# A state-space scan and a feed-forward block in one kernel: the first state products re-ordered, one weight step pulled ahead, one step of the second y put in one place

## The chip, the cores and the metric

The kernel runs on one core of a Trainium2 chip. The core has a matrix engine (TensorE, PE in the profile, with its weight loads as PEld), a vector engine (VectorE, DVE), a scalar engine (ScalarE, ACT), a general engine (GpSimd, POOL) and a queue engine that issues transfers (SyncE, SP). Each works through its own list in order and waits for others by semaphores. The metric is the device time of one execution in microseconds (us). Three timed executions of the kernel before gave 348.64, 349.24 and 348.39 us, so the median is 348.64 us.

## The reference

Two parts follow each other. The first is a chunked linear recurrence for 4 batches of 8 heads, 768 steps long, with head width 32 and state width 16. For each chunk of the sequence

```
M       = (C B^T) * exp(cum_i - cum_j), lower triangle       # inside the chunk
y_intra = M x
y_inter = (C state) * exp(cum_i)                             # from the state carried in
state   = exp(sum) * state + sum_j B_j x_j exp(cum_last - cum_j)
```

where `cum` is the running sum of log a. The second part takes y as 3072 rows of 256 numbers and computes `g = h / (1 + exp(-1.702 h))` with `h = y w_in` (256 to 2048), and then `g w_out` (2048 to 256). The two weight matrices arrive as 64-bit floats and are used as 32-bit ones; the kernel does this conversion itself.

## The kernel before, in words

The 3072 rows are cut into six groups of 512 rows (`g` = 0 to 5). A group is two pairs of 128-row chunks; the kernel works on chunks as two sides of 64 rows each (side 0 and side 1). For each group the kernel forms yT, the transposed y of the group (128 x 2 x 512, the two halves of the 256 columns are `t` = 0 and 1), then 16 hidden blocks of 128 columns, then the output. Group 0 uses plain products; from group 1 on, the kernel uses a scheme of seven products in place of eight (the lines L948, L958 and L1053), which does not change here.

**First y.** `finish(range(PG))` (L1207) forms y of group 0 out of two sums in four banks of the accumulator memory, `y0_0` to `y0_3`, one for each pair of side and column half: bank `2 t + i` holds side `i`, half `t`. `intra` (L830) adds M x; a filler product (`dense(4, ...)`, 256 columns, result unused) follows; `inter` (L810) adds C times the carried state. `inter` is made of small products with 32 rows and 64 columns. The four row groups `r` = 0 to 3 of the array hold two heads each, and `r // 2` is the column half `t`. ScalarE then copies each bank to yT (L856, four copies, t outer and side inner). The first hidden product needs both copies of half 0, the second those of half 1.

**Weights.** The 64-bit words of w_in and w_out come in pieces. `PIECES` 0 to 3 are two hidden blocks each (blocks 0 to 7), 4 and 5 four blocks each (8 to 11, 12 to 15), 6 to 9 are w_out. Each piece goes through

- `fields(i)` on VectorE (L192, L195): take the exponent and the mantissa out of the high word; it is the first step that needs the piece's transfer;
- `clamp(i)` on ScalarE (L203, L204): bring the exponent into range;
- `rounded(i)` on VectorE (L208): add the low word to the mantissa;
- `join(i)` on VectorE (L222 and L228): put sign, exponent and mantissa together and write the 32-bit weights. For piece 4 it is done in two halves, so that blocks 8 and 9 come before 10 and 11. After pieces 1 and 5, `join` also issues the transfer of piece 6 or 9.

`narrow(i)` (L235) is `rounded(i)`, then `fields(i + 1)`, then `join(i)`.

**Hidden blocks of group 0.** `hidden(0, f)` (L887) is four PE instructions (two products, each in two passes) into one bank of a ring of four (`bank`, L581, tag "ff"), then a Silu on ScalarE (L896) that empties it. With the allocations in program order, block 9 takes the bank that block 5 used. The table `in_hidden` (L1228 to L1236) says what is put behind which block: `narrow(4)` and then `clamp(5)` behind block 4, `narrow(5)` behind 6, `pick_a` (two ScalarE copies, L366) behind 6, `clamp(6)` and `fan_all` (PE, L412) behind 9, and so on. The lists of all engines are put in that program order by `in_order` (L21), so ScalarE does `clamp(5)` after the Silu of block 4 and before that of block 5.

**The second y.** `in_project` says the same for the output products of group 0 (L990, four instructions for each `f`). Behind the products before f = 9 stand `score` (L682) and `gain` (L713, the increments of the state) of the second group. `gain` writes a bank that `since_start` on VectorE (L667) must have read. `finish(pairs, (0,))` puts `inter` of group 1 ahead of f = 13 and `finish(pairs, (1,))` puts `intra` and the two copies to yT (L871) ahead of f = 15.

**fold_ident(1)** (L333) fills the second half of a constant that `decay` (L402) uses from group 1 on. It is one VectorE instruction.

Of the kernel before, what the change touches and what calls it, by code (L numbers as in the profile page):

```python
# [35 lines left out]
def kernel(  # L36
# [151 lines left out]
    def fields(i):  # L188
        hi, cols = bits[i][1], slice(0, PIECES[i][2] * DM)
        mantissa[i] = wide.tile([P, PN], U32, tag="m", name=f"m{i}")[:, cols]  # L190
        power[i] = wide.tile([P, PN], U32, tag="p2", name=f"p2{i}")[:, cols]
        nc.vector.tensor_scalar(out=power[i], in0=hi, scalar1=0x7FF00000, scalar2=None,  # L192
                                op0=ALU.bitwise_and)

        nc.vector.tensor_scalar(out=mantissa[i], in0=hi, scalar1=0x000FFFFF,  # L195
                                scalar2=0x00100000, op0=ALU.bitwise_and, op1=ALU.bitwise_or)
# [9 lines left out]
    def rounded(i):  # L206

        nc.vector.scalar_tensor_tensor(out=mantissa[i].bitcast(FP32), in0=bits[i][0],  # L208
                                       scalar=2.0 ** -32, in1=mantissa[i],
                                       op0=ALU.mult, op1=ALU.add)  # L210
# [4 lines left out]
    def join(i, parts=1):  # L215

        name, f, n = PIECES[i]
        n //= parts
        low, m, p2 = bits.pop(i)[1], mantissa.pop(i), power.pop(i)
        for k in range(parts):  # L220
            cols, fs = slice(k * n * DM, (k + 1) * n * DM), slice(f + k * n, f + (k + 1) * n)
            nc.vector.scalar_tensor_tensor(out=p2[:, cols], in0=low[:, cols], scalar=0x80000000,  # L222
                                           in1=p2[:, cols], op0=ALU.bitwise_and, op1=ALU.bitwise_or)
            if name == "in":
                dst, h = w_in[:, fs].rearrange("p f k e -> p (f k e)").unsqueeze(1), 1
            else:
                dst, h = w_out[:, :, fs].rearrange("p c f e -> p c (f e)"), 2
            nc.vector.scalar_tensor_tensor(  # L228
                out=dst, in0=m[:, cols].bitcast(FP32).rearrange("p (h e) -> p h e", h=h),
                scalar=2.0 ** -20, in1=p2[:, cols].bitcast(FP32).rearrange("p (h e) -> p h e", h=h),  # L230
                op0=ALU.mult, op1=ALU.mult)
        for n in NEXT.get(i, ()):
            fetch(n)

    def narrow(i):  # L235
        rounded(i)
        if i + 1 < len(PIECES):
            fields(i + 1)
        join(i, 2 if i == 4 else 1)


    scratch = dram.tile([NC, 2, NB * NH, H], FP32, name="scratch")
# [90 lines left out]
    def fold_ident(k, engine=nc.vector):  # L333

        engine.tensor_tensor(
            out=idents[:, k * NH:(k + 1) * NH],
            in0=ident[:, :H].unsqueeze(1).to_broadcast([P, NH, H]),
            in1=ident[:, H:].unsqueeze(1).to_broadcast([P, NH, H]), op=ALU.add)
# [41 lines left out]
    for i, n, head in ((0, 1, PG), (1, 2, PG), (0, 0, 1)):  # L380
        t = whose[32 * i:32 * i + 32, n:n + 1]
# [199 lines left out]
    def bank(name):  # L581
        return ps.tile([P, 4 * P], FP32, tag="ff", name=name)

    def area(name):
        return psa.tile([P, R, 4 * P], FP32, tag="cb", name=name)
# [202 lines left out]
    def finish(pairs, steps=range(2)):  # L788


        g, first = divmod(pairs[0], PG)
        early = pairs[0] < PG

        swap = g > 2
        if 0 in steps:
            if early:
                y = [bank(f"y0_{i}")[:, :2 * P].rearrange("p (k i) -> p k i", i=H) for i in range(4)]
                begun_y[0] = [[y[2 * t + i] for t in range(NK)] for i in range(2)], set()
            else:
                both = area(f"y{pairs[0]}")[:, :, :len(pairs) * 2 * H].rearrange(  # L800
                    "p (s t) (k i) -> p s t k i", s=2, i=H)
                begun_y[pairs[0]] = [[both[:, i, t] for t in range(NK)] for i in range(2)] + [both], set()
        y, begun = begun_y[pairs[0]]

        def begin(i, t, parts):
            new = not begun & {(i, t, q) for q in parts}
            begun.update((i, t, q) for q in parts)
            return new

        def inter(n, p, ts=range(2)):  # L810

            for k in range(2):
                for i in range(2):
                    m = 2 * k + i
                    if (4 * p + m) % (2 * NC) == 0:
                        continue
                    old = state[p][:, m - 1] if m else state[p - 1][:, 3]
                    for r in range(R):
                        t = r // 2
                        if t not in ts:  # L820
                            continue
                        half = r % 2 ^ (swap and i)
                        rows, to = slice(32 * r, 32 * r + 32), Q * D * half
                        nc.tensor.matmul(  # L824
                            out=y[i][t][to:to + Q * D, 2 * n + k], lhsT=old[rows],
                            rhs=st[p]["CsT"][rows, k, SIDES[i]],
                            start=begin(i, t, range(Q * half, Q * half + Q)), stop=early,
                            tile_position=(32 * r, to), skip_group_check=True)

        def intra(n, p):  # L830
            L = Ls[p]
            for k in range(2):
                for h in range(NH):
                    for i, side in enumerate(SIDES):
                        t, q = divmod(h, HB)
                        if i and swap:
                            q = (q + Q) % HB
                        nc.tensor.matmul(  # L838
                            out=y[i][t][D * q:D * q + D, 2 * n + k], lhsT=rx[p][side, k, h],
                            rhs=L[side, k, h // Q, h % Q],  # L840
                            start=begin(i, t, (q,)), stop=not early, tile_position=(H * i, D * q),
                            skip_group_check=True)

        cols = slice(2 * first * P, 2 * (first + len(pairs)) * P)

        if first == 0:
            yT[g] = ffn.tile([P, NK, TG], FP32, tag="yT", name=f"yT{g}")
        if early:
            for n, p in enumerate(pairs):
                intra(n, p)  # L850
            dense(4, area("idle")[:, 0])
            for t in range(NK):
                for n, p in enumerate(pairs):
                    inter(n, p, (t,))
                for i in range(2):
                    nc.scalar.activation(  # L856
                        yT[g][:, t, cols].rearrange("p (k s i) -> p s k i", s=2, i=H)[:, i], y[i][t],
                        AF.Copy)
        else:
            for step in steps:  # L860
                for n, p in enumerate(pairs):
                    (inter, intra)[step](n, p)
            if 1 not in steps:
                return
            o = yT[g][:, :, cols].rearrange("p t (k s i) -> p s t k i", s=2, i=H)
            for i in range(2):
                if i and swap:
                    for to, src in (SIDES, SIDES[::-1]):
                        nc.scalar.activation(o[to, i], y[2][src, i], AF.Copy)
                else:  # L870
                    nc.scalar.activation(o[:, i], y[2][:, i], AF.Copy)  # L871
        for p in pairs:
            state.pop(p - 1, None)
            st.pop(p)
            Ls.pop(p)
# [287 lines left out]
    def dense(n, t):  # L1163
        nc.tensor.matmul(out=t[:, :n * H], lhsT=ones,
                         rhs=ones[:, :H].unsqueeze(1).to_broadcast([P, n, H]),
                         start=True, stop=True, skip_group_check=True)
# [36 lines left out]
    keep_first()  # L1203
    dense(8, bank("dense"))
    finish(range(PG))
    join(0, 2)
    fields(1)  # L1207
    clamp(1)
    table(AF.Silu)
    rounded(1)  # L1210
    fold_ident(1)
    join(1)
    fields(2)
    clamp(2)
# [3 lines left out]
    def at(places, i, *work):  # L1218
        places.setdefault(i, []).extend(work)

    in_hidden = [{} for _ in range(NG)]
    in_project = [{} for _ in range(NG)]
# [10 lines left out]
    for i, k, c in ((2, 1, 1), (3, 2, 2), (4, 4, 4), (5, 6, 8), (6, 9, 12), (7, 12, 15)):  # L1233
# [3 lines left out]
    n, p = 2 * PG, 3 * PG  # L1237
    pairs = PG, PG + 1
# [5 lines left out]
    at(in_project[0], 5, lambda: narrow(9))  # L1244
    at(in_project[0], 9, lambda: score(pairs), lambda: gain(pairs), lambda: keep_both(pairs, True),
       lambda: weigh(PG), lambda: weigh(PG + 1))
    at(in_project[0], 13, lambda: finish(pairs, (0,)))
    at(in_project[0], 15, lambda: finish(pairs, (1,)))
    at(in_project[0], 13, lambda: mix_in(1), lambda: spread(n + 1, held=True),
       lambda: load(n + 1, "x"), lambda: mix_in(2), lambda: mix_in(3),  # L1250
       lambda: turn_blocks(2), lambda: decay(n))
# [92 lines left out]
    for g in range(2, NG):  # L1344
        n, p = (g + 1) * PG, (g + 2) * PG
# [103 lines left out]
```

## Time and profile before

| | |
|---|---|
| median of three timed executions | 348.64 us (348.39 to 349.24) |
| the profiled execution's own time | 350.11 us |
| its span, from first to last instruction | 348.0 us |
| mean granted TensorE clock | 1.000 |
| PE busy | 342.8 us, 99% of the span |
| PEld busy | 269.6 us, 77% |
| DVE busy | 254.0 us, 73% |
| ACT busy | 155.2 us, 45% |
| POOL busy | 13.1 us, 4% |
| first y: L838 at 13.82 us, L824 at 16.73 us | 56 instructions of L824 in 1.68 us |
| hidden blocks of group 0 | from 18.40 us on |
| second y: L824 at 74.23 us, L838 at 78.83 us | 56 instructions of L824 in 1.04 us |

A line of the timeline reads: start, length, engine, source line, operation, output and inputs with their sizes, number of instructions, and in brackets the idle time of the engine just before it and what ended it. Lengths of merged lines cover all their instructions. Because the matrix engine is pipelined, the share of 99% does not say that it is at its peak; what counts is how far apart its instructions start.

### The profile page before, as it was taken

The page shows a single profiled execution, that of the slowest core. Times are in us where ns is not written, and L with a number is a line of the kernel's source. Part 1 is how long each engine was busy: PE and PEld are TensorE (multiplying, and loading weights), DVE is VectorE, ACT ScalarE, POOL GpSimd, SP SyncE. Part 2 cuts the span into 40 slices and gives each one's busy share as a digit, 9 for nine tenths or more (in the row PEclk, how much of TensorE's full clock was granted, in tenths as well). Part 3 has the DMA queues.
Part 4 walks back from the last instruction along what each step waited for, and adds up shares of the span by engine and source line. Part 5 has one row for each costly group of instructions (what it writes and reads, how often), then busy time and mean ns, then how long its engine had stood idle before and what let it go on. Part 6 is the DMA issues. An engine that isn't in the chain of part 4 may idle for free.

```text
span 348.0 us, 8123 instructions
## 1 busy us (share of the span) xinstructions
PE 342.8 (99%) x3380; PEld 269.6 (77%) x3380; DVE 254.0 (73%) x479; ACT 155.2 (45%) x352; POOL 13.1 (4%) x42
## 2 busy tenths in 40 slices
PE   8999999999999999999999999999999999999996
PEld 6643444545688888888888888888888888899996
DVE  5899997999779999667997567788465654465463
ACT  4798675106453322754442454432564331554320
POOL 8300000100000100000000000000000000000000
PEclk9999999999999999999999999999999999999999
DMA  6598899535526200436704036400000300000301
GB/s 161 128 329 190 199 211 225 104 62 99 109 45 132 62 0 2 77 70 117 120 16 61 0 66 116 81 0 3 0 4 3 59 4 0 0 2 0 62 0 61
DMA packets 89980, 25.92 MB, mean 74 GB/s; under 512 B 73432, under 2 KB 87128, under 8 KB 89944
## 3 DMA queue, kind: packets, MB, share of 16 engines
q1 hardware_dynamic: 89112, 24.88, 33.7%
q10 hardware_dynamic: 832, 0.52, 0.6%
q8 instruction: 26, 0.43, 0.5%
q14 instruction: 10, 0.08, 0.1%
HBM read 22.15 MB, written 3.24 MB: 73 GB/s over the span
## 4 chain that ended last, share of the span: by engine, by line
PE 83%; DMA 7%; DVE 5%; SPq 2%; issue 2%; POOL 0%; ACT 0%; DVEq 0%
PE acc L1053 28%; PE X L948 19%; PE Y L958 14%; PE acc L1060 7%; PE o L990 4%; DMA bits<-in_moe_w_in_dram 3%; DMA af<-in_a_dram 3%; PE h L893 2%; PE y L838 2%; SPq L180 2%; PE cb L682 2%; PE y L824 1%; PE A L713 1%; DVE p L222 1%; PE ab L554 1%
## 5 line engine op out<-in xcount | busy, mean ns | idle before, releaser
L953 ACT ACTIVATE ac<-X 128x256 f32<-128x256 f32 x76 | 29.1, 383 | 81.4 <-PE X L948 80.7
L1080 DVE TENSOR_TENSOR gT<-Y,ac 128x512 f32<-128x512 f32 x38 | 26.2, 689 | 40.3 <-PE Y L958 32.5
L1053 PE MATMUL acc<-mg,mw 128*128 128x256 f32 x192 | 54.5, 379 | 0.0
L925 ACT ACTIVATE gT<-gT 128x512 f32<-128x512 f32 (+1 forms) x76 | 38.9, 519 | 29.4 <-DVE gT L1080 28.9
L948 PE MATMUL X<-my,mi 128*128 128x256 f32 x152 | 45.2, 380 | 0.0
L1053 PEld LDWEIGHTS acc<-mg,mw 128*128 128x128 f32 x192 | 36.5, 190 | 5.0
L1080 DVE TENSOR_TENSOR gT<-Y,b 128x256 f32<-128x256 f32 x38 | 15.8, 418 | 28.5 <-PE Y L958 28.5
L893 PE MATMUL h<-yT,w_in 128*128 128x512 f32 x80 | 35.8, 598 | 0.5 <-DVE w_in L228 0.4
L1053 PE MATMUL acc<-gT,w_out 128*128 128x256 f32 x128 | 35.5, 379 | 0.0
L948 PEld LDWEIGHTS X<-my,mi 128*128 128x128 f32 x152 | 28.0, 190 | 4.1 <-ACT ac L953 0.4
L893 PEld LDWEIGHTS h<-yT,w_in 128*128 128x128 f32 x80 | 14.7, 190 | 19.2 <-issue 15.6
L990 PE MATMUL o<-gT,w_out 128*128 128x512 f32 x64 | 28.6, 597 | 0.0
L916 DVE TENSOR_TENSOR mg<-gT 128x512 f32<-128x512 f32 x40 | 27.2, 681 | 0.0
L1053 PEld LDWEIGHTS acc<-gT,w_out 128*128 128x128 f32 x128 | 24.2, 190 | 3.4 <-ACT yT L871 0.2
L953 ACT ACTIVATE b<-X 128x256 f32<-128x256 f32 x38 | 14.6, 384 | 21.0 <-PE X L948 20.5
L948 PE MATMUL X<-yT,w_in 128*128 128x256 f32 x76 | 23.2, 389 | 0.0
L958 PE MATMUL Y<-yT,w_in 128*128 128x256 f32 x76 | 22.7, 381 | 0.0
L958 PE MATMUL Y<-my,mi 128*128 128x256 f32 x76 | 22.7, 380 | 0.0
L958 PE MATMUL Y<-yT,mi 128*128 128x256 f32 x76 | 22.5, 379 | 0.0
L948 PE MATMUL X<-my,w_in 128*128 128x256 f32 x76 | 22.4, 379 | 0.0
L990 PEld LDWEIGHTS o<-gT,w_out 128*128 128x128 f32 x64 | 11.8, 190 | 13.2 <-issue 12.4
L402 DVE TENSOR_TENSOR_SCAN L<-a,idents 128x1024 f32<-128x1024 f32 x9 | 20.5, 2277 | 0.4 <-DMA a<-scratch 0.4
(159 smaller groups left out, 548.0 us busy)
## 6 DMA issues: line engine op xcount, KB each, us to landing
a<-scratch SPq DMA_DIRECT2D x18, 256.0 KB, 5.0
bits<-in_moe_w_out_dram SPq DMA_DIRECT2D x8, 512.0 KB, 5.7
x<-in_x_dram SPq DMA_DIRECT2D x24, 128.0 KB, 3.1
out_dram<-ob SPq DMA_DIRECT2D x40, 64.0 KB, 1.9
bits<-in_moe_w_in_dram SPq DMA_DIRECT2D x8, 256.0 KB, 4.7
bits<-in_moe_w_in_dram SPq DMA_DIRECT2D x4, 512.0 KB, 11.2
b<-in_B_dram SPq DMA_DIRECT2D x20, 64.0 KB, 3.1
af<-in_a_dram SPq DMA_DIRECT2D x3, 384.0 KB
```

The costliest lines, as they stand in the source:

```text
L180: nc.sync.dma_start(out=dst[k], in_=src[k])
L402: nc.vector.tensor_tensor_scan(out=L, data0=ra[p].rearrange("p k e -> p (k e)"), data1=idents.rearrange("p h i -> p (h i)"), initial=0.0, ...
L893: nc.tensor.matmul(out=h, lhsT=w_in[:, f, k], rhs=yT[g][:, k], start=(k == 0), stop=(k == NK - 1), skip_group_check=True)
L916: nc.vector.tensor_tensor(out=t[:, 0:2], in0=B[:, :, 1], in1=B[:, 0], op=ALU.subtract)
L925: nc.scalar.activation(o, i, AF.Silu, scale=GELU_SCALE)
L948: nc.tensor.matmul(out=s["X"], lhsT=lhsT, rhs=rhs, start=i == "1", stop=i == "4", skip_group_check=True)
L953: nc.scalar.activation(copy, s["X"], AF.Copy)
L958: nc.tensor.matmul(out=o, lhsT=lhsT, rhs=rhs, start=s.pop("new", False), stop=i != "5", skip_group_check=True)
L990: nc.tensor.matmul(out=o[c], lhsT=w_out[:, c, f], rhs=gT[g, f // 2][:, f % 2], start=(f == 0), stop=(f == NF - 1), skip_group_check=True)
L1053: nc.tensor.matmul(out=acc[g][0][i][:, cols], lhsT=w, rhs=h[:, cols], start=(j == 0 and k == 0 and (i, 0) in begins), stop=(j == NF // 2 - ...
L1060: nc.tensor.matmul(out=o[k] if type(o) is list else o[:, cols], lhsT=h[:, cols], rhs=w, start=(j == 0 and (i, k) in begins), stop=(j == NF ...
L1080: nc.vector.tensor_tensor(out=o, in0=v, in1=w, op=ALU.add)
```

## The change

Four edits. In `narrow(4)`, `join(4)` is put ahead of `fields(5)`. In `finish` for the first group, the state products are ordered by side (both pairs of side 0, then both of side 1, each time over all four row groups) where they were ordered by column half before, the filler is 192 columns wide in place of 256, and all four copies stand behind the products. `fold_ident(1)` moves from behind `rounded(1)` to ahead of `fields(1)`. `finish` of group 1 stands in one piece ahead of f = 15.

```diff
     def narrow(i):
         rounded(i)
+        if i == 4:
+            join(i, 2)
         if i + 1 < len(PIECES):
             fields(i + 1)
-        join(i, 2 if i == 4 else 1)
+        if i != 4:
+            join(i)
...
-        def inter(n, p, ts=range(2)):
+        def inter(n, p, sides=range(2)):
 
             for k in range(2):
-                for i in range(2):
+                for i in sides:
                     m = 2 * k + i
                     if (4 * p + m) % (2 * NC) == 0:
                         continue
                     old = state[p][:, m - 1] if m else state[p - 1][:, 3]
                     for r in range(R):
                         t = r // 2
-                        if t not in ts:
-                            continue
                         half = r % 2 ^ (swap and i)
...
         if early:
             for n, p in enumerate(pairs):
                 intra(n, p)
-            dense(4, area("idle")[:, 0])
+            dense(3, area("idle")[:, 0])
+            for i in range(2):
+                for n, p in enumerate(pairs):
+                    inter(n, p, (i,))
             for t in range(NK):
-                for n, p in enumerate(pairs):
-                    inter(n, p, (t,))
                 for i in range(2):
                     nc.scalar.activation(
                         yT[g][:, t, cols].rearrange("p (k s i) -> p s k i", s=2, i=H)[:, i], y[i][t],
...
     join(0, 2)
+    fold_ident(1)
     fields(1)
     clamp(1)
     table(AF.Silu)
     rounded(1)
-    fold_ident(1)
     join(1)
...
-    at(in_project[0], 13, lambda: finish(pairs, (0,)))
-    at(in_project[0], 15, lambda: finish(pairs, (1,)))
+    at(in_project[0], 15, lambda: finish(pairs))
```

## The prediction

> **What bounds the kernel now.** I read the page first, then the timeline by engine around each of the four edits, and last the stretch from there to the next point at which the matrix engine waits. The page says that PE is the engine to follow.
>
> ```profile
> span 348.0 us, 8123 instructions
> PE 342.8 (99%) x3380; PEld 269.6 (77%) x3380; DVE 254.0 (73%) x479; ACT 155.2 (45%) x352; POOL 13.1 (4%) x42
> ```
>
> So a step is worth what it takes off PE's own list, or off a wait of PE that no later wait gives back. The timeline of the first y and the first hidden blocks:
>
> ```profile
> 16.10 0.70 PE L1164 MATMUL idle<-ones 128*128 128x256 f32 x2
> 16.73 1.68 PE L824 MATMUL y<-CsT,S 32*64 32x64 f32 x56
> 17.69 1.30 ACT L856 ACTIVATE yT<-y 128x256 f32<-128x256 f32 x4 [1.05 <-PE y L824]
> 18.46 0.43 DVE L192 TENSOR_SCALAR p<-bits 128x512 uint32<-128x512 uint32 x1 [0.61 <-DMA bits<-in_moe_w_in_dram]
> 18.92 0.72 ACT L203 ACTIVATE p<-p,edge 128x512 f32<-128x512 uint32 x1
> 19.68 0.72 ACT L204 ACTIVATE p<-p,edge 128x512 uint32<-128x512 f32 x1
> 20.56 0.68 DVE L222 SCALAR_TENSOR_TENSOR p<-bits,p 128x512 uint32<-128x512 uint32 x1
> ```
>
> Then weight piece 5, for which VectorE waits, and behind it the wait of PE at block 8:
>
> ```profile
> 28.44 1.22 DVE L208 SCALAR_TENSOR_TENSOR m<-bits,m 128x1024 f32<-128x1024 uint32 x1
> 30.33 0.69 DVE L192 TENSOR_SCALAR p<-bits 128x1024 uint32<-128x1024 uint32 x1 [0.67 <-DMA bits<-in_moe_w_in_dram]
> 31.06 1.15 ACT L203 ACTIVATE p<-p,edge 128x1024 f32<-128x1024 uint32 x1 [1.13 <-DVE p L192]
> 31.54 0.69 DVE L222 SCALAR_TENSOR_TENSOR p<-bits,p 128x512 uint32<-128x512 uint32 x1
> 32.24 1.15 ACT L204 ACTIVATE p<-p,edge 128x1024 uint32<-128x1024 f32 x1
> 33.10 3.67 PE L893 MATMUL h<-yT,w_in 128*128 128x512 f32 x8 [0.45 <-DVE w_in L228]
> 33.29 1.06 ACT L896 ACTIVATE gT<-h 128x512 f32<-128x512 f32 x2
> ```
>
> The row at 33.29 is the one to see: it holds the Silus of blocks 5 and 6. Block 5's products were done by about 29, but its Silu stands behind both `clamp(5)` rows. The last view is the second y:
>
> ```profile
> 65.98 0.42 DVE L667 TENSOR_TENSOR CsT<-tp,since 128x256 f32<-128x256 f32 x1
> 66.02 1.22 PE L713 MATMUL A<-x,Be 64*32 64x64 f32 x56
> 66.46 0.61 PEld L713 LDWEIGHTS A<-x,Be 64*32 64x32 f32 x54 [0.31 <-DVE CsT L667]
> 74.23 1.04 PE L824 MATMUL y<-CsT,S 32*64 32x64 f32 x56
> 85.59 0.84 PE L713 MATMUL A<-x,Be 64*32 64x64 f32 x56
> ```
>
> At 66 us PE waits for VectorE in the middle of `gain`; the same 56 instructions at 85.59 take 0.84 us.
>
> **The change part by part.** The times below are those of the profiled execution (350.11 us, of which 348.0 is span); the difference is put on the median, 348.64.
>
> *First y by sides.* The filler loses 64 of 256 columns. Between the filler rows of 512 columns (12.77 us, 1.13) and 256 (0.70) lie 0.43 us, so 64 columns are 0.11 and the products begin at 16.62. Its cover holds: the state copies of ScalarE end at 16.63 (15.68 + 0.95), and only the third set of products reads the later one. Now the four row groups follow each other. The row at 74.23 is such an order: 56 instructions in 1.04 us, four starting 0.007 us apart and the next four 0.058 later; the row at 16.73 has two and two, 1.68 us. That saves 0.64, and the products end at 17.66, not 18.41. But all copies now stand behind them: side 0 of half 0 is done early, side 1 of half 0 starts at 17.70, ends at 18.08, and block 0 starts at 18.13 instead of 18.40. So 0.75 becomes 0.27. The fourth copy ends at 18.64, ahead of `clamp(1)` at 18.92, which waits for VectorE: ScalarE is not later.
>
> A rule of the skill speaks against this. The Trainium skill, TensorEngine Tiling (Array Packing), section Restrictions and Gotchas, says that different row tiles cannot access one accumulator bank at the same time; row groups 0 and 1 share a bank here, and so do 2 and 3. The row at 74.23 has the same sharing and starts all four within 0.02 us, so the trace does not bear the rule out for these shapes; what its case would cost is worked out among the rivals.
>
> *fold_ident.* It takes 0.60 us of VectorE's list (19.95 to 20.56). Put at 17.77, where VectorE has 0.61 us of idle time before piece 1 lands, it is free. `join(1)` then follows `rounded(1)` directly, but it needs `clamp(1)`, which ends at 20.40; so L222 starts at 20.45, not 20.56. Blocks 2 and 3 get their weights 0.11 earlier and block 2 starts at 22.00 instead of 22.11. PE, at 18.13, would be there by 21.67: of its 0.27 only 0.11 passes. The bounds are 0 (VectorE no earlier) and 0.11; I take 0.11, since `clamp(1)` is a row of its own. Both lists run 0.11 earlier from here.
>
> *join(4) ahead of fields(5).* `rounded(4)` now starts at 28.33, and `join(4)` at 29.46 (1.13 between such starts), filling the wait for piece 5. Its four steps take 2.66 (31.54 to 34.20). Blocks 8 and 9 have weights at 30.87, so block 8 starts without a wait: 32.49 - 0.11 = 32.38, not 33.10 (PE's starts are 0.43 apart, and the last before the wait was at 32.06). That is 0.72 earlier.
>
> But `fields(5)` moves from 30.33 to 32.12, though its data is there, and what is queued behind it is ScalarE: `clamp(5)` at 32.85 (0.73 after `fields(5)` starts, as at 31.06) and 34.03, the Silu of block 5 from 35.08 to 35.66. Block 9 needs that bank. It would be due at 32.38 + 4 x 0.43 = 34.10, and starts at 35.71; before it started at 34.89. Restarting after a wait costs 0.08 (0.51 to the next start instead of 0.43, as after 33.10). So from block 10 on PE is 0.82 + 0.08 = 0.90 later. The bounds are -0.80 (no wait at block 9; 0.11 + 0.61 + 0.08) and +0.90; I take the upper, because the order of ScalarE's list and the ring of four leave no other bank. `pick_a` ends at 36.95, ahead of `fan_all` at 37.60, and the next Silus are done at 37.4 and 37.9 for blocks due at 38.9 and 40.7: no second wait. VectorE itself is earlier (L353 at 33.34, not 34.20). `join(4)` issues no transfer; SP's list at that time waits on its own landings, and POOL's holds nothing moved.
>
> *At 66 us.* PE comes to `gain` at 66.92 instead of 66.02. L667 ends at 66.41 as before: VectorE's row at 56.65 waits for piece 9, whose transfer SP issues at 48.7 after its own queue, and its list is full from there. So the wait disappears: 1.22 becomes 0.84, -0.38. The bounds are 0 and -0.38; the row at 85.59 is the nearest. PE is now +0.52.
>
> *Second y in one place.* A run of L990 products is left and entered once instead of twice: a first product takes 0.53 instead of 0.43, and entering a small-tile product 0.52 instead of 0.43. `inter` and `intra` directly after each other cost the same 0.15 as `inter` and L990 (150.99, the later groups). That saves 0.10 + 0.09, together 0.20 with rounding; bounds 0 and 0.20. The copies stand behind `intra` as before, and SP's wait for `intra` (row at 79.72) is 0.3 later, ahead of data due after 85.
>
> The sum: -0.80 + 1.70 (the wait at block 9 with its restart, 1.61 + 0.08) - 0.38 - 0.20 = +0.32. Between there and the end PE is its own bound; the next VectorE step that it needs (85.17 + 0.49) has gained slack. Span 348.3, profiled 350.4, median 348.64 + 0.32 = 348.96 us.
>
> **The rivals.**
>
> *The gain passes.* If block 9 does not wait, PE is 0.80 earlier at 66 us. For it: one wait of PE in the profile, 0.45 us, is plainly removed. Against it: the Silu at 33.29. Even then L667 holds PE until 66.46, and only the 0.20 remain: 348.44. If that chain moves as well, -1.00: 347.64.
>
> *Pieces land earlier in the timed runs: slower.* The profiled execution is 1.47 us longer than the median, and it may be transfers. If piece 5 lands by 29.57 (0.76 earlier), VectorE before has no wait, block 8 before starts at 32.49 and block 9 at 34.21, while block 9 after still starts at 35.71, since that is set by VectorE's list alone. If L667 is also ahead of PE (1.07 earlier), nothing is absorbed: 1.50 + 0.08 - 0.20 = +1.38, 350.02. Against it: no row shows where the 1.47 lies, and part may be outside the span.
>
> *The four row groups do not run next to each other.* Then the products last until 18.30, the fourth copy ends at 19.28, `clamp(1)` starts 0.36 later, and so does all up to block 9: +0.68, 349.32. The row at 74.23 speaks against it. This is what the skill's rule above would give.
>
> **How the numbers follow.** Chances: forecast 0.50, gain passes 0.16, earlier landing 0.28, row groups 0.06. A change of 0.3% is 1.05 us, about what a measurement of this kernel can tell from no change. Faster: 0.02 of the forecast and 0.10 of the gain, 0.12. Slower: 0.06 of the forecast (if 66 us absorbs nothing and VectorE is no earlier, 0.32 + 0.38 + 0.11 = 0.81, and a little more), 0.25 of the landing, 0.01 of the row groups, 0.32. Same: 0.56. The range is 348.2 (below the held gain) to 350.1 (the landing case); it leaves out most of the faster cases and a tail above, about 0.2. The forecast's own range is 348.4 to 349.5.
>
> **What would show it.** Right: L824 at 16.62 with about 1.04 for 56; block 0 at 18.13; L222 of piece 1 at 20.45; no wait for w_in at 32.4; PE idle about 1.2 to 1.6 us ahead of 35.7, ended by ScalarE's L896; 56 instructions of `gain` in 0.84 near 67; one run of L824 and L838 near 79. Wrong: block 9 on time, `clamp(5)` ahead of 32, or PE still held at 66 us.

## The result, and the profile after

Timed against each other on one chip, the changed kernel took 350.37 us (median; 349.85 to 351.45) and the kernel before 348.39 us (348.11 to 349.55). The ratio is 1.0053 with a 95% interval of 1.0033 to 1.0073, which is 1.85 us (1.15 to 2.54) on 348.4. So the change makes the kernel slower by over 0.3%. The forecast was 348.96 us, +0.32 on the median known then (348.64), and its range ended at 350.1: the time lies just outside it.

The two profiled executions alone do not show this. The page of the changed kernel:

```profile
span 347.9 us, 8122 instructions
PE 340.4 (98%) x3380; PEld 268.2 (77%) x3380; DVE 254.2 (73%) x479; ACT 155.3 (45%) x352; POOL 13.4 (4%) x42
```

Its span is 0.1 us shorter than the one before, while the timed difference is 1.85. The execution profiled here took 349.85 us, the lowest of its kernel's times; that of the kernel before took 350.11, which is 1.7 above the median of the timed executions. Comparing the two spans would have given the wrong answer. The stretches within them can still be compared. Two rows of PE in the kernel before, and then the timeline of PE in the changed kernel, in the order of the prediction's steps:

```profile
18.40 14.26 PE L893 MATMUL h<-yT,w_in 128*128 128x512 f32 x32
...
36.70 0.69 PE L412 MATMUL ab<-X,ones 32*64 32x256 f32 x16
```

```profile
15.76 0.59 PE L1166 MATMUL idle<-ones 128*128 128x192 f32 x2
16.29 1.04 PE L825 MATMUL y<-CsT,S 32*64 32x64 f32 x56
17.80 3.70 PE L895 MATMUL h<-yT,w_in 128*128 128x512 f32 x8 [0.47 <-ACT yT L858]
21.70 12.32 PE L895 MATMUL h<-yT,w_in 128*128 128x512 f32 x28 [0.20 <-DVE w_in L228]
35.48 1.98 PE L895 MATMUL h<-yT,w_in 128*128 128x512 f32 x4 [1.47 <-ACT gT L898]
37.40 0.69 PE L415 MATMUL ab<-X,ones 32*64 32x256 f32 x16
...
66.72 0.79 PE L716 MATMUL A<-x,Be 64*32 64x64 f32 x56
```

The filler starts 0.34 us earlier in this execution than in the one before, ahead of anything that the change touches, so places are read as distances. From filler to block 0 are 2.04 us, where 2.30 were: the first y gives 0.26. At 21.70 PE waits 0.20 us for the weights of block 2. The wait at block 8 is gone, and PE stands 1.47 us ahead of block 9, released by ScalarE's Silu. The row at 37.40 is `fan_all`, behind block 9; from block 0 to it are 19.60 us, where 18.30 were (18.40 to 36.70). From `fan_all` to `gain` are 29.32 us in both kernels (36.70 to 66.02 before), so nothing is given back between them. At `gain` PE is no longer held. VectorE and ScalarE in the same execution show where the 1.47 comes from:

```profile
29.24 0.68 DVE L222 SCALAR_TENSOR_TENSOR p<-bits,p 128x512 uint32<-128x512 uint32 x1
...
31.89 0.69 DVE L192 TENSOR_SCALAR p<-bits 128x1024 uint32<-128x1024 uint32 x1
32.62 1.15 ACT L203 ACTIVATE p<-p,edge 128x1024 f32<-128x1024 uint32 x1 [3.02 <-DVE p L192]
...
34.85 1.07 ACT L898 ACTIVATE gT<-h 128x512 f32<-128x512 f32 x2
```

`join(4)` starts at 29.24, `fields(5)` not before 31.89. ScalarE stands for 3.02 us at the head of `clamp(5)`, and the Silus of blocks 5 and 6 (34.85) stand behind it. Block 9 needs the bank that the first of them empties. The second y, in one piece:

```profile
77.94 1.04 PE L825 MATMUL y<-CsT,S 32*64 32x64 f32 x56
...
80.32 1.98 PE L992 MATMUL o<-gT,w_out 128*128 128x512 f32 x4
```

From its first small product to the output products behind it are 2.38 us. Before, they were 6.02 (74.23 to 80.25) with eight output products of 0.43 between the parts, 2.58 without these:

```profile
74.23 1.04 PE L824 MATMUL y<-CsT,S 32*64 32x64 f32 x56
75.20 3.70 PE L990 MATMUL o<-gT,w_out 128*128 128x512 f32 x8
78.83 1.48 PE L838 MATMUL y<-L,x 64*32 64x64 f32 x128
80.25 1.98 PE L990 MATMUL o<-gT,w_out 128*128 128x512 f32 x4
```

The stretches also show why the two spans are alike. The changed kernel lost 1.30 us in the ten blocks (19.60 for 18.30), and got back 0.26 at block 0, 0.43 at `gain` and 0.20 at the second y: a loss of 0.4 by the change, close to the forecast. The rest is of this pair of executions: its filler started 0.34 earlier, and from the `gain` near 85 us to the one near 128 us it took 42.58 us for 42.82.

### The profile page after: what moved, and what is told of

Its sections match the earlier page's. It is cut to its first block, busy times and chain, and to the rows that moved or that the text cites. A ratio compares the mean times of both kernels' runs of the same rounds, so it can differ in the third digit from the quotient of the medians.

```text
span 347.9 us, 8122 instructions
## 1 busy us (share of the span) xinstructions
PE 340.4 (98%) x3380; PEld 268.2 (77%) x3380; DVE 254.2 (73%) x479; ACT 155.3 (45%) x352; POOL 13.4 (4%) x42
## 4 chain that ended last, share of the span: by engine, by line
PE 89%; DMA 6%; SPq 2%; DVE 1%; POOL 1%; issue 1%; ACT 0%; DVEq 0%; ACTq 0%
PE acc L1055 28%; PE X L950 19%; PE Y L960 14%; PE o L992 8%; PE acc L1062 7%; PE h L895 6%; DMA bits<-in_moe_w_in_dram 4%; PE y L839 2%; SPq L180 2%; PE cb L685 2%; PE y L825 1%; PE A L716 1%; DMA b<-in_B_dram 1%; DMA az<-in_a_dram 1%; POOL CsT L670 0%
```

## The experiments

Each kernel is one edit away from the kernel before or from the changed kernel (join_gain_free, join_late5 and best are two), and was timed against the kernel before on the same chip. The chips differ between experiments, so the ratios are compared, and medians only where two kernels ran on one chip. In the last column of this table stands the ratio, with its interval. The two columns ahead of it come from one profiled execution of each: the ten hidden blocks (start of block 0 to start of `fan_all`, us) and how long PE was held in `gain` beyond the 0.79 us that the 56 instructions take unheld.

| kernel | ten blocks | held at `gain` | ratio to before |
|---|---|---|---|
| before, first profile | 18.30 | 0.4 | 1 |
| same_before | 17.54 | 0.8 | 1.0001 [0.9984, 1.0018] |
| sides_alone | 17.44 | 0.1 | 0.9996 [0.9971, 1.0021] |
| fold_alone | 17.75 | 0 | 1.0010 [0.9985, 1.0035] |
| merge_alone | 17.62 | 0 | 0.9994 [0.9970, 1.0017] |
| no_join | 18.36 | 0 | 0.9988 [0.9964, 1.0012] |
| gain_free | 17.45 | removed | 0.9997 [0.9976, 1.0017] |
| join_alone | 19.18 | 0 | 1.0046 [1.0031, 1.0061] |
| join_gain_free | 19.18 | removed | 1.0040 [1.0016, 1.0064] |
| after | 19.60 | 0 | 1.0053 [1.0033, 1.0073] |
| clamp_behind6 | 17.59 | 0.2 | 0.9978 [0.9963, 0.9992] |
| best | 18.51 | removed | 0.9982 [0.9966, 0.9999] |
| late5 | 18.39 | 0 | 1.0020 [0.9998, 1.0041] |
| join_late5 | 20.49 | 0 | 1.0074 [1.0050, 1.0099] |

### The kernel before a second time

> The kernel before, unchanged, as one more profiled execution. Landing theory (in ordinary executions the weight pieces land earlier than in the profile shown, so that the kernel before has neither the wait at block 8 nor the one in gain): time equal to before (348.4), and in the trace fields(5), L192 on VectorE, starts by 29.7 us and not at 30.33, block 8 waits less than 0.2 us and gain (L713 near 66 us) takes about 0.84 us and not 1.22. Other-parts theory (the profile shown is an ordinary execution, and the loss comes from the first y, fold_ident or the second y): both waits are there as shown, 0.6 us at block 8 and 0.3 us in gain.

Measured: 349.47 us against 349.51, ratio 1.0001. The edit is none; only the profile is new. The timeline of PE in that execution:

```profile
18.33 17.60 PE L893 MATMUL h<-yT,w_in 128*128 128x512 f32 x40
35.87 0.69 PE L412 MATMUL ab<-X,ones 32*64 32x256 f32 x16
...
65.19 0.30 PE L713 MATMUL A<-x,Be 64*32 64x64 f32 x2
66.01 0.77 PE L713 MATMUL A<-x,Be 64*32 64x64 f32 x54 [0.53 <-DVE CsT L667]
```

All forty instructions of the ten blocks are one row: no wait at block 8. It was there in the first profile (0.45 idle ahead of 33.10), and the same code runs here without it. Piece 5 was there when VectorE came (L192 at 29.40, no wait); in the first profile it was not (30.33, behind 0.67 us of waiting). The hold at `gain` is there in both: here the 56 instructions last from 65.19 to 66.78, which is 0.80 more than the 0.79 of an unheld run. So each expectation was half right in this execution: block 8's wait was not there, the hold was.

### `join(4)` ahead of `fields(5)`, alone and taken back

In the kernel before, for join_alone, and taken back in the changed kernel, for no_join:

```diff
     def narrow(i):
         rounded(i)
+        if i == 4:
+            join(i, 2)
         if i + 1 < len(PIECES):
             fields(i + 1)
-        join(i, 2 if i == 4 else 1)
+        if i != 4:
+            join(i)
```

> The kernel before with join(4) ahead of fields(5) and nothing else. Landing theory: PE waits about 1.5 us at block 9 for ScalarE, nothing gives it back, so +1.4 to +1.7 us (about 350.0), slower than the whole change would be without its 0.2 of the second y. Other-parts theory: +0.5 us (0.90 + 0.11 - 0.38 of the prediction's terms, without what fold_ident gave and the second y), about 348.9.

> The changed kernel with join(4) put back behind fields(5). Landing theory: the three other edits gain 0.1 to 0.3 us, so 348.1 to 348.3, ratio 0.999. Other-parts theory: they hold most of the loss, +1.0 to +1.4 us, about 349.6.

Measured: join_alone 350.98 us, 1.0046, which is +1.6 us (1.1 to 2.1); no_join 349.04 us, 0.9988, -0.4 us (-1.3 to 0.4). So this edit carries the loss, and the rest of the change is no more than its measurement can tell from nothing. PE in join_alone:

```profile
18.54 15.80 PE L896 MATMUL h<-yT,w_in 128*128 128x512 f32 x36
35.80 1.98 PE L896 MATMUL h<-yT,w_in 128*128 128x512 f32 x4 [1.46 <-ACT gT L899]
37.72 0.69 PE L415 MATMUL ab<-X,ones 32*64 32x256 f32 x16
```

Blocks 0 to 8 run as one row, and then comes the same wait as in the changed kernel. In no_join it is gone, and block 8 waits for its weights, as in the first profile (the timeline of VectorE and PE):

```profile
30.19 0.69 DVE L192 TENSOR_SCALAR p<-bits 128x1024 uint32<-128x1024 uint32 x1 [0.53 <-DMA bits<-in_moe_w_in_dram]
32.96 3.67 PE L892 MATMUL h<-yT,w_in 128*128 128x512 f32 x8 [0.34 <-DVE w_in L228]
```

### `clamp(5)` behind the Silus of blocks 5 and 6

In the changed kernel; nothing is moved on VectorE.

```diff
-    at(in_hidden[0], 6, lambda: pick_a(PG))
+    at(in_hidden[0], 6, lambda: clamp(5), lambda: pick_a(PG))
...
-        at(in_hidden[0], c, lambda i=i: clamp(i + 1))
+        if i != 4:
+            at(in_hidden[0], c, lambda i=i: clamp(i + 1))
```

> The changed kernel with clamp(5) behind the Silus of blocks 5 and 6 on ScalarE, ahead of pick_a, where it stood ahead of both. It takes away the wait of block 9 and leaves join(4) ahead of fields(5). If ScalarE's order is the cause, PE's 1.47 us of idle time ahead of block 9 goes to under 0.2, and the time to 348.1 to 348.5 (under either theory by about 1.5 us less than the changed kernel). If another part costs the time, the wait goes and the time stays at 349.5 or more.

Measured: 349.02 us, 0.9978, which is -0.8 us (-1.3 to -0.3): faster than the kernel before, and 1.96 below join_alone on the same chip by the medians. The timeline of PE and ScalarE:

```profile
17.88 17.53 PE L895 MATMUL h<-yT,w_in 128*128 128x512 f32 x40 [0.47 <-ACT yT L858]
...
28.20 1.55 ACT L898 ACTIVATE gT<-h 128x512 f32<-128x512 f32 x3
30.30 0.60 ACT L898 ACTIVATE gT<-h 128x512 f32<-128x512 f32 x1 [0.55 <-PE h L895]
32.28 1.15 ACT L203 ACTIVATE p<-p,edge 128x1024 f32<-128x1024 uint32 x1 [1.39 <-DVE p L192]
```

`clamp(5)` still waits for VectorE (at 32.28; 32.62 in the changed kernel), but four Silus stand ahead of it now, where two did, and forty instructions of PE are one row. VectorE's order is that of the changed kernel, so the loss is made by what is queued behind `clamp(5)` on ScalarE, and not by `fields(5)` being late. The kernel that this one is a single edit away from, the changed kernel, had 1.0053 on its chip.

### The hold at `gain`, with and without the join

One more copy on ScalarE (0.39 us), so that L667 of the second chunk pair of group 1 reads its own copy and the bank that `gain` writes is not held. In the kernel before, for gain_free, and with the join edit above as well, for join_gain_free.

```diff
-        if 2 in steps and p < PG:
+        if 2 in steps and p == PG + 1:
```

> The kernel before with one more ScalarE copy (L590, 128x256, about 0.4 us where ScalarE is idle): VectorE's L667 for the second chunk pair reads that copy, and gain on PE no longer waits for L667 but for ScalarE at about 61 us. Theory that PE is held at gain in ordinary executions (0.38 us in the profile shown, 0.53 us in the second one): time 0.3 to 0.8 us under before, gain in about 0.79 us. Theory that a later wait takes the place of this one: the wait goes and the time stays within 0.2 us of before.

> join(4) ahead of fields(5) and the same extra copy. If the hold at gain gave back a part of the wait at block 9 in join_alone, then the step from gain_free to this one is larger than the 0.46% from before to join_alone: about 1.8 to 2.1 us (the 1.58 of block 9, less what block 8 waited, plus nothing given back). If the hold gives nothing back, both steps are alike, 1.6 us.

Measured: gain_free 349.02 us, 0.9997, -0.1 us (-0.8 to 0.6); join_gain_free 350.54 us, 1.0040. The step between the two is 1.5 us by the medians (0.43% by the ratios), against 1.6 for the join edit where the hold may be present. If the hold had given back 0.38 of the loss in ordinary executions, its removal alone would have gained that, and the join would have cost 0.38 more without it. Neither shows, but an effect of this size would not stand out in these intervals either, so the timing leaves it open. In the profile the edit did what it was to do (PE):

```profile
17.79 17.52 PE L893 MATMUL h<-yT,w_in 128*128 128x512 f32 x40
...
64.56 0.81 PE L713 MATMUL A<-x,Be 64*32 64x64 f32 x56
```

and block 8 does not wait here either. From block 0 to `fan_all` (35.24) are 17.45 us, the ten blocks with no wait.

### The other three edits, each alone

In the kernel before each: sides_alone takes the first y's new order with the shorter filler, merge_alone the second y in one place, fold_alone moves `fold_ident(1)`. Their cores are

```diff
-            dense(4, area("idle")[:, 0])
-            for t in range(NK):
+            dense(3, area("idle")[:, 0])
+            for i in range(2):
                 for n, p in enumerate(pairs):
-                    inter(n, p, (t,))
+                    inter(n, p, (i,))
+            for t in range(NK):
```

```diff
-    at(in_project[0], 13, lambda: finish(pairs, (0,)))
-    at(in_project[0], 15, lambda: finish(pairs, (1,)))
+    at(in_project[0], 15, lambda: finish(pairs))
```

```diff
+    fold_ident(1)
     fields(1)
     clamp(1)
     table(AF.Silu)
     rounded(1)
-    fold_ident(1)
     join(1)
```

> The kernel before with only the first y by sides and the filler of 192 columns. By the prediction: the products take 1.04 us instead of 1.68, block 0 starts 0.27 us earlier against the filler, and block 2 waits for the weights of piece 1, so that nothing passes: 0.0 us, at most -0.27. If the order by sides costs time (row groups that share a bank, or the copies), +0.3 us or more.

> The kernel before with only finish of group 1 in one place. By the prediction -0.20 us (one run of small products less to enter and leave), 0.9994. If the products, now ahead of the copies to yT, delay what follows: +0.3 us or more.

> The kernel before with only fold_ident(1) moved. By the prediction L222 of piece 1 starts 0.11 us earlier and block 2 with it: 0 to -0.11 us, not to be told from before. If it delays fields(1) instead, up to +0.6 us.

Measured: 348.48 us (0.9996), 348.68 us (0.9994) and 349.06 us (1.0010). None can be told from no change. In the trace of sides_alone the filler starts at 15.68 and block 0 at 17.71, 2.03 apart, as in the changed kernel, and the 56 products take 1.04 us. Here the gain passes, where the expectation was that nothing does, since block 2 does not wait for its weights:

```profile
17.71 17.51 PE L892 MATMUL h<-yT,w_in 128*128 128x512 f32 x40 [0.47 <-ACT yT L855]
35.15 0.69 PE L412 MATMUL ab<-X,ones 32*64 32x256 f32 x16
```

From the filler to `fan_all` are 19.47 us, and 19.76 in gain_free, which has the old order and no wait. fold_alone shows something that the prediction missed. The first row of piece 1 on VectorE in merge_alone, where `fold_ident` stands in its old place, and then `fold_ident` and the same row in fold_alone:

```profile
17.45 0.42 DVE L192 TENSOR_SCALAR p<-bits 128x512 uint32<-128x512 uint32 x1
```

```profile
17.82 0.68 DVE L335 TENSOR_TENSOR idents<-ident 128x512 f32<-128x512 f32 x1
18.42 0.42 DVE L192 TENSOR_SCALAR p<-bits 128x512 uint32<-128x512 uint32 x1
```

The idle 0.61 us that was to cover the moved step is a wait for piece 1's transfer. In merge_alone VectorE has none: piece 1 was there, and a `fold_ident` ahead of it would put off `fields(1)` by 0.60. So it is in sides_alone, gain_free, join_alone and join_gain_free, too. In fold_alone piece 1 landed at 17.30, ahead of `fold_ident`, and L222 of piece 1 starts 4.59 us behind the filler, where merge_alone and gain_free have 4.29: the move costs 0.30 there.

### A later piece 5

In the kernel before (late5), and with the join edit as well (join_late5): the transfer of piece 5 is issued behind those of `az`.

```diff
-    for i in range(2, 6):
+    for i in range(2, 5):
         fetch(i)
     rows_a(az, (nc.sync,))
+    fetch(5)
```

This was to make the wait for piece 5 certain, and so to test the order that the change chose under the condition that would favour it.

> The kernel before with the transfer of piece 5 issued behind that of az (lines 1198 to 1200), and nothing else; by the profile shown it would land near 32 us instead of 29.4 to 30.2. If block 8's wait in the kernel before is set by that landing, fields(5) starts near 32, block 8 waits 1.5 to 2.5 us and the kernel takes 1 to 2 us longer (349.9 or more).

> The same late transfer with join(4) ahead of fields(5). fields(5) would start at 31.9 to 32.2 in any case, so the late landing costs little: block 8 has no wait, block 9 waits 1.5 to 1.9 us, and the time stays within 0.4 us of join_alone (+1.6 us over before). Against late5 it would be equal or up to 0.8 us faster: the sign of this edit then hangs on the landing of one transfer. If the edit costs time in another way, it stays 1.5 us above late5.

Measured: late5 350.09 us, 1.0020, which is +0.7 us (-0.1 to 1.4) where 1 to 2 were expected, and join_late5 351.82 us, 1.0074, which is +2.6 us (1.7 to 3.5) and more than the 0.4 above join_alone's +1.6 that was expected. The condition was not made. VectorE in late5:

```profile
26.42 0.69 DVE L192 TENSOR_SCALAR p<-bits 128x1024 uint32<-128x1024 uint32 x1 [0.73 <-DMA bits<-in_moe_w_in_dram]
...
30.27 0.71 DVE L192 TENSOR_SCALAR p<-bits 128x1024 uint32<-128x1024 uint32 x1
```

The second row is piece 5, and it does not wait: its last transfer was issued at 22.33 us (18.48 in the first profile of before) and landed at 30.14 (30.21 there). The first is piece 4, issued ahead of the moved transfers, and VectorE waits for it. PE in join_late5 waits in two places:

```profile
30.06 5.39 PE L896 MATMUL h<-yT,w_in 128*128 128x512 f32 x12 [0.77 <-DVE w_in L228]
37.21 1.98 PE L896 MATMUL h<-yT,w_in 128*128 128x512 f32 x4 [1.76 <-ACT gT L899]
```

The step between the two kernels is 1.7 us by the medians, as without the edit. Whether a truly late piece 5 makes the new order pay was not tried and stays open.

### `clamp(5)` moved and `gain` not held

best is the changed kernel with both edits, that of clamp_behind6 and that of gain_free.

> The changed kernel with clamp(5) behind the Silus of blocks 5 and 6 and the extra ScalarE copy ahead of gain: all of the change's gains without the wait of block 9 or the hold at gain. 0.5 to 1.0 us under before, ratio 0.9975; about 2 us under the changed kernel.

Measured: 348.49 us, 0.9982, -0.6 us (-1.2 to 0). It just beats the kernel before, and it is no better than clamp_behind6 as far as the two intervals tell. Its profiled execution shows why one execution is not enough (PE):

```profile
25.55 10.54 PE L895 MATMUL h<-yT,w_in 128*128 128x512 f32 x24 [0.52 <-DVE w_in L228]
36.40 0.69 PE L415 MATMUL ab<-X,ones 32*64 32x256 f32 x16 [0.31 <-ACT X L369]
```

and VectorE:

```profile
23.32 0.43 DVE L192 TENSOR_SCALAR p<-bits 128x512 uint32<-128x512 uint32 x1 [0.71 <-DMA bits<-in_moe_w_in_dram]
```

Here piece 3 was late. `fields(3)` waited 0.71 us for its transfer, `join(2)` stands behind it in VectorE's list, and so block 4 waited for its weights: the pattern that the change removed for piece 5. No such wait is in the profile of clamp_behind6, whose code is the same up to there. The wait at 36.40 is a price of the moved `clamp(5)`, which stands ahead of `pick_a` (L369) on ScalarE: with VectorE late, `fan_all` waits here.

## Why the prediction was wrong

The direction was right, +0.32 us, and so was the mechanism of the loss. On the two profiled executions even the size was nearly right, 0.4 us as worked out above. On the timed ones it was not, because the two largest gains set against the loss were waits of one execution, and most executions profiled since do not have them.

*First y by sides.* Right in its parts: 56 instructions in 1.04 us (1.04 forecast), block 0 earlier by 0.26 from the filler on (0.27 forecast; 0.27 in sides_alone). The four row groups do start next to each other, 0.007 us apart, so the rival in which the products take 1.68 falls. The rule behind that rival, that different row tiles cannot access one accumulator bank at the same time (the Trainium skill, TensorEngine Tiling (Array Packing), section Restrictions and Gotchas), does not show in these starts. That little of the gain passes was right for the changed kernel: block 2 waits for its weights, and block 9 starts 19.72 us after the filler, in join_alone and join_gain_free 19.56. It is not so in each kernel: in sides_alone, where piece 1 was there in time, all of it reaches `fan_all`.

*`fold_ident`.* No gain. Its cover, 0.61 us of waiting for piece 1, is gone in five of the other executions. In the changed kernel piece 1's L222 starts 4.46 us behind the filler, as in the first profile of before, where the forecast was 0.11 earlier; in fold_alone it is 0.30 later.

*`join(4)` ahead of `fields(5)`.* The wait at block 9 was forecast at 1.61 with 0.08 for the restart, 1.69 in all, and came as it was described: released by L898, behind `clamp(5)`, with no second wait. In join_alone and join_gain_free the ten blocks take 19.18 us, which is 1.73 above the 17.45 of gain_free, where nothing waits. clamp_behind6 and no_join show that it is the cause, since each takes the wait away and with it the loss.

**The step that failed is the -0.80 set against it.** Of this, 0.69 was block 8's wait with its restart, to be removed. The seven profiled executions with `fields(5)` in its old place (the upper part of the table) have 17.44 to 18.36 us for the ten blocks, 17.78 in the mean, 0.33 above the undisturbed 17.45. That 0.33 is the most that the new order can remove in the mean of these profiles (a part of it, as in fold_alone, is no wait at block 8); the first profile of before, at 18.30, is the second longest of the seven. It is a real wait (no_join has it as well, and there too piece 5 was late), but the other five of the seven do not have it. The 0.11 in the same term is the gain of `fold_ident`, which did not come.

**The second term that failed is the -0.38 at `gain`.** The hold was read as always present and always given back. In the profiles it is 0.4, 0.8, 0.1 and three times 0 for the kernels that can have it and `fields(5)` in its old place (upper part of the table), 0.2 in the mean. gain_free measures -0.1 us for its removal, with an interval (-0.8 to 0.6) that excludes neither.

With these credits left out, the prediction's terms are 0.32 + 0.69 + 0.11 + 0.38 = +1.50. With the means of the profiles in their place, the ten blocks of the changed kernel (19.60 - 17.78), block 0 (-0.26), the hold (-0.23) and the second y (-0.20) give +1.1. The timed +1.85 (1.15 to 2.54) holds the first, and the second, 1.13, lies just below its lower end; the +1.6 (1.1 to 2.1) of join_alone holds 19.18 - 17.78 = 1.40.

The profiled execution of the changed kernel was the lowest of its times, 0.52 below their median. The fourteen profiles show where another execution can be longer. From `fan_all` to `gain` PE takes 29.3 us in every one, and from the `gain` near 128 us to the end 219.6. What moves is the start of block 0 (17.71 to 18.63 us), the ten blocks, the hold, and the stretch from the `gain` near 85 us to that near 128 us, 42.58 to 43.12, in which PE waits for ScalarE in some (in same_before it stands 0.18 us ahead of L948 at 118.90, released by ScalarE's L953). The prediction took PE to be its own bound from `gain` to the end, and in these executions it is not. The changed kernel's profile has the shortest of these stretches, 42.58, and an early block 0. How much of each an ordinary execution has, and why the changed kernel came out above the second sum, is not settled closer than that.

*Second y in one place.* Right: forecast -0.20 by the pieces; the trace has 2.58 and 2.38 us, -0.20. From `gain` to the first hidden product of the next group, the hold taken off, the profiles with this edit have 15.4 us, and those without it 15.6. The timed ratio of merge_alone (0.9994) can neither show nor deny it.

*The rivals.* "Pieces land earlier in the timed runs" came nearest: +1.38 by its sum, +1.85 (1.15 to 2.54) measured. It was given 0.28 because no row showed where the 1.47 us between the profiled execution and the median lay, and a part might have been outside the span. Little was: an execution's time is 1.7 to 2.2 us above its span in all of these runs, 2.1 in that one. A second profile of the same kernel lacks block 8's wait, though that execution, too, took 349.86. Against gain_free, profiled at 347.90, the first profile is longer by 0.6 us at the start of block 0, 0.85 in the ten blocks, 0.4 at `gain` and 0.2 behind 85 us. How the median execution divides them stays open. "The gain passes" did not come, and needs the edit of clamp_behind6: with it, the kernel is 0.8 us (0.3 to 1.3) faster than before, which goes with the 0.20 to 1.00 that this rival gave.

## What to carry to other kernels

A wait that ends with a transfer is a wait of that execution: compare the profiled execution's own time with the median first, and set such a wait against a cost only with its mean over several profiles, since the cost here came from lists alone and was there each time (1.46 to 1.76 us of waiting at block 9 in four profiles). When a step is moved ahead of another on one engine, find who waits for the one that is now late, and what stands behind that waiting instruction in its engine's list; here moving that one too (`clamp(5)` behind two Silus) turned +0.5% into -0.2%. A gain ahead of a wait that another engine's list ends, as the first y's 0.26 us in the changed kernel, is not added to the sum.

## What was not expected of the hardware

The landing of transfers moves between executions of the same code. The last transfer of piece 5, issued at 18.48 us, landed at 30.21 in the first profile of the kernel before; in the second it was issued at 18.89 and landed at 29.23. Over the twelve kernels that issue the pieces as before, that landing lies between 27.63 us (gain_free) and 30.29 (join_alone). The start of the first y's filler moves as well, 15.48 to 16.33 us over all fourteen, though no edit stands ahead of it; what moves it was not looked for. With `az` put in front of piece 5, VectorE waited 0.73 us (late5) and 1.24 us (join_late5) for piece 4, which is issued ahead of both, and 0 to 0.16 in the other twelve profiles, while piece 5 landed no later in late5 than in the first profile of before. Two executions do not show that the order of issue is the cause.
